# One fused attention and gated MLP kernel: block-diagonal M and z, statistics' loads in buffers of their own, first blocks' loads issued first

## The chip, the cores and the metric

The kernel runs on one core of one Trainium2 chip. The metric is device time in microseconds; lower is better. The version before was run three times: 676.85, 678.36 and 680.79 us, median 678.36 us. All inputs are float32 or float64 in HBM; the weights of the MLP are float64.

## The reference

Attention of 4 batches, 8 heads, 576 rows, 64 columns per head, mixed with a linear-attention memory, and then a gated MLP over 2304 rows of 512:

```python
scores = where(causal, -1e9, q @ k.T / sqrt(64))
a = exp(scores - max);  a /= a.sum(-1) + 1e-09
local = a @ v
q_p = where(q > 0, q, exp(q) - 1) + 1
mem_out = (q_p @ M_prev) / ((q_p @ z_prev) + 1e-06)
x = sigmoid(beta) * mem_out + (1 - sigmoid(beta)) * local
# rows of x are 8 heads x 64
xn = x / sqrt(mean(x * x) + 1e-06) * rms_g
g = xn @ w_gate
out = (silu(g) * (xn @ w_val)) @ w_out
```

## The kernel before

The 2304 rows are 18 blocks of 128. Blocks 0 and 1 are the first 128 rows of batch 0 and of batch 1; they need no earlier keys and are computed wholly in float32 (`n < NA`). All other blocks use float16 pairs (a high and a low half), whose scales come from statistics over k and v of a whole batch. Blocks go in pairs (chunks) through the MLP: `m_proj` multiplies a chunk's transposed, normalised rows `xT` with 12 column groups F of the weights; `m_act` makes the gated product; `m_down` multiplies with w_out. Chunk 0 is done in float32, with weights that were only just turned from float64 to float32.

The order on each engine is that of a scheduler at build time, which takes the calls in program order and with priorities (`tc.high_priority`). An engine runs its own list strictly in that order; so does SP, the queue that issues nearly all DMAs. Each DMA takes the next of eight semaphores, and waits for the DMA that had that semaphore before it.

What happens in the head of the program, with the names used below:

- `HORD` is a string that orders the first loads: q0 and k0 (`kv`, k and v) of block 0, M0 and M1 (the memory of batch 0 and 1, each loaded twice, into both halves of the partitions), w0 and w1 (the first weight pieces). `HP` is a priority for them; 0 is none.
- Weights: gate and val come in 24 pieces of 128 x 512 float64 (512 KB). `load_w` puts piece p in slot p mod 5 of a ring in the `wo` tile, and `paced` lets it start only once the conversion of piece p - 3 has begun. `f64_to_f32` converts a piece: one operation on ACT (L777), then two on DVE (L778, L779). A slot is free for piece p + 5 after the second one on DVE. w_out follows in 12 pieces of the same kind.
- `prep_qk32` transposes k and q of a block on PE (L351, `tp`), `phi_calc` makes phi(q), `prep_phi32` transposes it.
- `u_scores` multiplies q and k (L411, `sc`), `u_exp` takes the exponentials on ACT with their sums in `den`, `u_lo` transposes the result (L351 again, from `S`), `pv32` multiplies it with v (L582, `both<-kv`).
- `mem32` makes for each of 8 heads a product of 64 partitions with z (L558, `zn`, one column) and one with M (L570, `both<-wo`, 64 columns). `evac32` scales both by the two denominators and adds them; `x_norm` and `x_float` (L691, `xtp`) normalise and transpose the row block for the MLP.
- `all_stats(b)` for batches 0 and 1: `stat_blk` feeds each block's k and v to `gram` (L147, `csum<-kv`, `csum<-pre`), four products of 128 x 128 each, whose maximum DVE reads (L241). The blocks (b, 2) and (b, 3) are loaded for this alone by `load_pre`, into the tile `pre`; there is one buffer for it (`tag="res", bufs=1`). So each of these four loads (two DMAs each) waits until the products of the one before it are done.
- `gv_scales` uses the same `gram` on converted weights (`csum<-wgv`).

Of the kernel before, what the change touches and what calls it, by code (L numbers as in the profile page):

```python
# [9 lines left out]
F32 = mybir.dt.float32  # L10
F16 = mybir.dt.float16
# [5 lines left out]
ALU = mybir.AluOpType  # L17
# [4 lines left out]
LNP = 15.0 * math.log(2.0)  # L22
XSCALE = 2.0 ** 11
NEG = -1.0e38
HP = 0
HORD = "q0 k0 M0 w0 w1 q1 k1 M1"
LAG = 3
LAG0 = 8
NA = 2
HEAD0 = 1.0  # L30
ADD32 = "p"
# [27 lines left out]
def attn_memory_moe_kernel(  # L59
# [12 lines left out]
    nc = tc.nc  # L72
    B, D, H = M_prev.shape[:3]
# [158 lines left out]
    def stat_blk(b, i):  # L232
        if b < 2:
            r = slice(0, P) if i < NI else slice(b * TR, b * TR + TR)
            src = pre.pop((b, i)) if (b, i) in pre else stage[blk_of[(b, i)] if i < NI else NI * 2]
            for j in range(2):
                if i == 0:
                    csum["kv", b, j] = ps.tile([P, 512], F32, tag="out", name=f"csum{j}")
                gram(csum["kv", b, j], src[r, j], i == 0, i == NI)
                if i == NI:  # L240
                    nc.vector.tensor_reduce(  # L241
                        stt[b][:, j, 0:1], csum.pop(("kv", b, j))[:, :P], axis=AX.X, op=ALU.max
                    )
            return
        if i < NI:
            for j in range(2):
                square_acc(stage[blk_of[(b, i)]][:, j], stt[b][:, j, i : i + 1])
# [145 lines left out]
    def group(n):  # L393
        return max(1, 4 // (blocks[n][1] + 1)) if blocks[n][1] < 2 else 1
# [71 lines left out]
    def u_exp(n, h0):  # L466
        s, w, nm = Ssb[(n, h0)]
        G = group(n)
        if n < NA:
            if h0 % 4 == 0:  # L470
                den[n, h0 // 4] = tiny.tile([P, 2, 4], F32, tag="qsc", name="den", bufs=5)
            for g in range(G):
                v_ = s[:, g * w : (g + 1) * w]
                nc.scalar.activation(
                    v_, v_, AF.Exp, bias=nm[:, g : g + 1], scale=-1.0,
                    accum_out=den[n, h0 // 4][:, 1, (h0 + g) % 4 : (h0 + g) % 4 + 1],
                )
# [68 lines left out]

    t1s = {}

    def mem32(n, g4):

        b, i = blocks[n]
        if g4 == 0:
            z = ps.tile([P, 2, 4], F32, tag="sc", name="zn")
            for x in range(H):
                h, r = head32(x)
                if x % 4 == 0:
                    zt = z if x == 0 else ps.tile([P, 2, 4], F32, tag="sc", name="zn")
                nc.tensor.matmul(  # L558
                    zt[:, x // 4, x % 4 : x % 4 + 1], q32[n][r, 1, h // 2, :],
                    zz[r, b * H + h : b * H + h + 1], start=True, stop=True,  # L560
                )
                if x % 4 == 3:
                    nc.vector.scalar_tensor_tensor(
                        out=den[n, x // 4][:, 0], in0=zt[:, x // 4], scalar=1e-6,
                        in1=gsig[:, 0, four(n, x // 4)], op0=ALU.add, op1=ALU.mult,
                    )
        accs[n, g4] = ps.tile([P, 2, 4, D], F32, tag=f"a{g4}", name=f"both{n}_{g4}", bufs=1)
        for x in range(4 * g4, 4 * g4 + 4):
            h, r = head32(x)
            nc.tensor.matmul(  # L570
                accs[n, g4][:, 0, x % 4], q32[n][r, 1, h // 2, :], qst[("M", b)][r, h * D : h * D + D],
                start=True, stop=True,
            )
        if (n, g4) == (NA - 2 + b, 1):
            del held["M", b, 1]

    def pv32(n, h0, pt):
        b, i = blocks[n]
        for g in range(group(n)):
            x = h0 + g  # L580
            h = head32(x)[0]
            nc.tensor.matmul(  # L582
                accs[n, x // 4][:, 1, x % 4], pt[:, g, :], stage[blk_of[(b, 0)]][:, 1, h * D : h * D + D],
                start=True, stop=True,
            )

    def evac32(n, g4):
        f = den.pop((n, g4))
        nc.vector.scalar_tensor_tensor(
            out=f[:, 1], in0=f[:, 1], scalar=1e-9,  # L590
            in1=gsig[:, 1, four(n, g4)], op0=ALU.add, op1=ALU.mult,
        )
        nc.vector.reciprocal(f, f)
        if g4 == 0:
            t1s[n] = sb.tile([P, H, D], F32, tag="t1", name=f"t1_{n}")
        t2 = sb.tile([P, 2, 4, D], F32, tag="t2", name=f"t2_{n}", bufs=1)
        nc.vector.tensor_tensor(
            t2, accs.pop((n, g4)), f.unsqueeze(3).to_broadcast([P, 2, 4, D]), ALU.mult
        )
        (nc.vector if ADD32 == "d" else nc.gpsimd).tensor_tensor(  # L600
            t1s[n][:, four(n, g4), :], t2[:, 0], t2[:, 1], ALU.add
        )

    def mem_mm(n, g4):
        if n < NA:
            return mem32(n, g4)
        b, i = blocks[n]
        if g4 == 0:
            t1s[n] = sb.tile([P, H, D], F32, tag="t1", name=f"t1_{n}")
# [141 lines left out]

    def load_pre(b, i):

        pre[(b, i)] = sb.tile([P, 2, HD], F32, tag="res", name=f"pre{b}_{i}", bufs=1)
        for j in range(2):
            nc.sync.dma_start(out=pre[(b, i)][:, j], in_=qkv[blk_of[(b, i)], :, j, :])

    def load_wo(f):
        at = {0: 7, 1: 9, 2: 11, 3: 7, 4: 9, 5: 11, 7: 9, 9: 11}.get(f)
# [279 lines left out]
            load_w(*pcs[p])  # L1039
    load_kv(2), load_kv(3)  # L1040
    setup_consts()
    for n in range(2):
        prep_qk32(n)
        phi_calc(n)
        prep_phi32(n)
# [223 lines left out]
```

## Time and profile before

| what | value |
|---|---|
| median of 3 runs | 678.36 us (676.85 to 680.79) |
| span of the profiled execution | 677.3 us |
| PE busy | 623.5 us, 92% |
| DVE busy | 474.8 us, 70% |
| ACT busy | 384.1 us, 57% |
| POOL busy | 164.3 us, 24% |
| HBM read and written | 36.20 MB, 4.72 MB |

The profiled execution has no time of its own in the list of runs; its span is 1.1 us under the median of the runs, and this difference stands for what lies around a span. The page cuts the span in 40 slices of 16.9 us: PE's busy share is 5, 8, 9, 8, 9 tenths in the first five, and the granted TensorE clock is 9, 6, 5, 5, 8 tenths there; in the second half of the span both are at 9 nearly throughout.

### The profile page before, as it was taken

The page shows a single profiled execution, that of the slowest core. Times are in us where ns is not written, and L with a number is a line of the kernel's source. Part 1 is how long each engine was busy: PE and PEld are TensorE (multiplying, and loading weights), DVE is VectorE, ACT ScalarE, POOL GpSimd, SP SyncE. Part 2 cuts the span into 40 slices and gives each one's busy share as a digit, 9 for nine tenths or more (in the row PEclk, how much of TensorE's full clock was granted, in tenths as well). Part 3 has the DMA queues.
Part 4 walks back from the last instruction along what each step waited for, and adds up shares of the span by engine and source line. Part 5 has one row for each costly group of instructions (what it writes and reads, how often), then busy time and mean ns, then how long its engine had stood idle before and what let it go on. Part 6 is the DMA issues. An engine that isn't in the chain of part 4 may idle for free.

```text
span 677.3 us, 16070 instructions
## 1 busy us (share of the span) xinstructions
PE 623.5 (92%) x6152; PEld 489.4 (72%) x6152; DVE 474.8 (70%) x1448; ACT 384.1 (57%) x799; POOL 164.3 (24%) x239
## 2 busy tenths in 40 slices
PE   5898968899798969999899899989999999999997
PEld 4786857755686647778687777767787788887774
DVE  5556977897899776689668666877887676872221
ACT  3334655647778776665657656956557554542322
POOL 0001110131255324232143122522232221212111
PEclk9655988899999969999899999999999999999999
DMA  7745899933933777636466763285785454351001
GB/s 257 271 165 198 253 273 249 208 72 63 226 76 76 170 161 167 142 76 146 112 139 111 167 161 64 51 153 135 124 135 114 90 93 99 76 76 21 32 1 31
DMA packets 191660, 88.63 MB, mean 131 GB/s; under 512 B 174176, under 2 KB 174176, under 8 KB 191584
## 3 DMA queue, kind: packets, MB, share of 16 engines
q1 hardware_dynamic: 191136, 87.59, 56.2%
q8 instruction: 48, 0.79, 0.5%
q14 instruction: 28, 0.23, 0.1%
q10 hardware_dynamic: 448, 0.02, 0.0%
HBM read 36.20 MB, written 4.72 MB: 60 GB/s over the span
## 4 chain that ended last, share of the span: by engine, by line
PE 56%; DMA 19%; DVE 11%; ACT 7%; issue 4%; SPq 2%; POOL 1%; ACTq 0%; DVEq 0%; POOLq 0%
PE gv L858 26%; DMA PT<-P 6%; PE out L920 4%; PE out L921 4%; PE out L919 4%; DMA wo<-in_moe_w_out_dram 3%; DMA kv<-in_qkv_dram 3%; PE sc L418 3%; PE sc L445 2%; ACT junk L225 2%; DVE S L424 2%; DMA wo<-in_moe_w_gate_dram 2%; DMA qT<-row 2%; DVE P L500 1%; DMA wo<-in_moe_w_val_dram 1%
## 5 line engine op out<-in xcount | busy, mean ns | idle before, releaser
L858 PE MATMUL gv<-xT,wgv 128*128 128x256 f16 x2304 | 314.5, 274 | 1.3 <-DMA xT<-x 1.3
L858 PEld LDWEIGHTS <-wgv 128*128 128x128 f16 x2304 | 221.9, 98 | 38.4 <-DMA xT<-x 1.5
L890 POOL TENSOR_TENSOR h<-th,h 128x256 f16<-128x256 f32 x96 | 72.4, 754 | 263.1 <-ACT h L889 202.8
L482 ACT ACTIVATE S<-S,nm 128x256 f32<-128x256 f32 (+4 forms) x128 | 75.1, 608 | 47.9 <-DVE nm L432 34.6
L418 PE MATMUL sc<-kT,qT 128*128 128x128 f16 x608 | 84.1, 221 | 4.5 <-DMA qT<-qT 1.8
L500 DVE TENSOR_TENSOR P<-S,P 128x512 f16<-128x512 f32 (+2 forms) x84 | 64.6, 769 | 26.3 <-ACT P L487 25.7
L874 ACT ACTIVATE th<-gv,wt 128x256 f32<-128x256 f32 x96 | 44.8, 467 | 57.4 <-PE gv L858 53.4
L875 DVE SCALAR_TENSOR_TENSOR th<-th,gv 128x256 f32<-128x256 f32 x96 | 39.9, 415 | 52.7 <-ACT th L874 52.1
L424 DVE CUSTOM_DVE_ANT_0 S<-sc,mask,qsc 128x256 f32<-128x256 f32 (+3 forms) x112 | 62.2, 573 | 17.6 <-PE sc L418 14.1
L920 PE MATMUL out<-wo,h 128*128 128x512 f16 x192 | 73.2, 382 | 0.4 <-DVE wo L98 0.4
L921 PE MATMUL out<-wo,h 128*128 128x512 f16 x192 | 72.3, 381 | 0.0
L919 PE MATMUL out<-wo,h 128*128 128x512 f16 x192 | 72.1, 382 | 0.0
L487 ACT CAST P<-S 128x512 f16<-128x512 f32 (+2 forms) x100 | 59.6, 596 | 12.1 <-DMA PT<-P 10.8
L526 PE MATMUL loc<-v,PT 128*128 128x65 f16 x304 | 50.2, 195 | 14.3 <-DMA PT<-P 14.1
L889 ACT CAST h<-th 128x256 f16<-128x256 f32 x96 | 38.4, 400 | 43.9 <-DVE th L878 42.0
L418 PEld LDWEIGHTS <-qT 128*128 128x128 f16 x608 | 51.2, 98 | 10.6 <-issue 3.4
L851 PE MATMUL gv<-xT,wgv 128*128 128x256 f32 x192 | 47.8, 405 | 6.0 <-DVE h32e L878 6.0
L527 PE MATMUL loc<-v,PT 128*128 128x64 f16 x304 | 50.0, 195 | 0.0
L528 PE MATMUL loc<-v,PT 128*128 128x65 f16 x304 | 50.0, 195 | 0.0
L878 DVE SCALAR_TENSOR_TENSOR th<-th,wt,gv 128x256 f32<-128x256 f32 x96 | 45.8, 477 | 1.7
L660 POOL TENSOR_TENSOR t<-t,t 128x256 f32<-128x256 f32 x32 | 25.8, 806 | 86.0 <-DVE t L656 73.5
L851 PEld LDWEIGHTS gv<-xT,wgv 128*128 128x128 f32 x192 | 37.7, 202 | 12.3 <-DVE h32e L878 6.4
(216 smaller groups left out, 1141.5 us busy)
## 6 DMA issues: line engine op xcount, KB each, us to landing
kv<-in_qkv_dram SPq DMA_DIRECT2D x36, 256.0 KB, 3.6
wo<-in_moe_w_gate_dram SPq DMA_DIRECT2D x12, 512.0 KB, 5.5
wo<-in_moe_w_val_dram SPq DMA_DIRECT2D x12, 512.0 KB, 5.3
q<-in_qkv_dram SPq DMA_DIRECT2D x18, 256.0 KB, 3.0
wo<-in_moe_w_out_dram SPq DMA_DIRECT2D x8, 512.0 KB, 4.6
qT<-qT SPq DMA_DIRECT2D x32, 128.0 KB, 2.4
out_dram<-res SPq DMA_DIRECT2D x16, 256.0 KB, 2.3
pre<-in_qkv_dram SPq DMA_DIRECT2D x8, 256.0 KB, 3.0
```

Of the source, the lines that this page charges most:

```text
L418: nc.tensor.matmul(t[:, g * w + j * P : g * w + (j + 1) * P], qT[n][:, t2, h, :], kT[blk_of[(b, j)]][:, h, :], start=(t2 == 0), stop=(t2 = ...
L424: nc.vector.tensor_tensor_reduce(out=s[:, g * w : (g + 1) * w], in0=t[:, g * w : (g + 1) * w], in1=mask[:, m0 : m0 + w], scale=qsc[n][:, 5 ...
L482: nc.scalar.activation(v_, v_, AF.Exp, bias=nm[:, g : g + 1], scale=-1.0)
L487: nc.scalar.copy(p16[:, : G * w], s[:, : G * w])
L500: eng.tensor_tensor(p16[:, w : 2 * w], s[:, :w], p16[:, :w], ALU.subtract)
L526: nc.tensor.matmul(a, phi_, vhi, start=(j == 0), stop=False)
L851: nc.tensor.matmul(o, wgv[:, 1 + p, o0 : o0 + P], xT[0][:, cc, :], start=(cc == 0), stop=(cc == NC - 1))
L858: nc.tensor.matmul(o, lhs, xT[c][:, rhs, :], start=(cnt == 0), stop=(cnt == 3 * NC - 1))
L890: nc.gpsimd.tensor_tensor(h16[:, 1], th, h16[:, 0], ALU.subtract)
L919: nc.tensor.matmul(o, hh, whi, start=(f == 0), stop=False)
L920: nc.tensor.matmul(o, hh, wlo, start=False, stop=False)
L921: nc.tensor.matmul(o, hl, whi, start=False, stop=(f == NF - 1))
```

## The change

Four things are changed.

- **Loads.** `pre` gets a tile per load of k and of v, in the ten buffers of `v16`, which are empty at that time, so that none of its eight DMAs waits for a product. `HORD` now orders q0, k0, q1, k1, M0, M1, w0, w1, w2, with a high priority.
- **Statistics.** The `gram` products of batches 0 and 1 get a lower priority (-300).
- **Memory.** `pair_memory` clears on POOL a tile `Mpair` of 128 x 1024 floats and a `zpair` of 128 x 16, and `pair_M` copies M of two heads at a time onto the diagonal. `mem32` then needs 4 products with 128 partitions and 128 columns in place of 8, and 4 with z in place of 8, and does its scaling alone (`fm32`).
- **Accumulators.** Memory and local part of a float32 block lie in separate PSUM tiles, `evac32` scales only the local part, and adds it to `t1`.

```diff
-HP = 0
-HORD = "q0 k0 M0 w0 w1 q1 k1 M1"
+HP = 3000
+HORD = "q0 k0 q1 k1 M0 M1 w0 w1 w2"
...
-                gram(csum["kv", b, j], src[r, j], i == 0, i == NI)
+                with tc.high_priority(-300):
+                    gram(csum["kv", b, j], src[j][r], i == 0, i == NI)
...
+    def pair_memory():
+        mb = sb.tile([P, 2, NC, 2, D], F32, tag="xT", name="Mpair")
+        zb = sb.tile([P, 2, NC, 2], F32, tag="h16", name="zpair", bufs=4)
+        nc.gpsimd.memset(mb, 0.0)
+        nc.gpsimd.memset(zb, 0.0)
...
+    def pair_M(b):
+        m4 = qst["M", b].rearrange("p (c t e) -> p c t e", c=NC, t=2)
+        for t, r in ((0, slice(0, D)), (1, slice(D, 2 * D))):
+            nc.gpsimd.tensor_copy(pairs["M"][r, b, :, t, :], m4[r, :, t, :])
...
+        for c in range(NC):
             nc.tensor.matmul(
-                accs[n, g4][:, 0, x % 4], q32[n][r, 1, h // 2, :], qst[("M", b)][r, h * D : h * D + D],
-                start=True, stop=True,
+                acc[:, 2 * c : 2 * c + 2, :], q32[n][:, 1, c, :], pairs["M"][:, b, c], start=True, stop=True
             )
+        for c in range(NC):
+            nc.tensor.matmul(
+                z[:, 2 * c : 2 * c + 2], q32[n][:, 1, c, :], pairs["z"][:, b, c], start=True, stop=True
+            )
...
-        pre[(b, i)] = sb.tile([P, 2, HD], F32, tag="res", name=f"pre{b}_{i}", bufs=1)
+        pre[(b, i)] = []
         for j in range(2):
-            nc.sync.dma_start(out=pre[(b, i)][:, j], in_=qkv[blk_of[(b, i)], :, j, :])
+            t = sb.tile([P, H, VW], F16, tag="v16", name=f"pre{b}_{i}_{j}", bufs=10)
+            t = t.bitcast(F32).rearrange("p a b -> p (a b)")[:, :HD]
+            nc.sync.dma_start(out=t, in_=qkv[blk_of[(b, i)], :, j, :])
```

SP's list before, from its start, loads alone. The tile `wo` holds M and the weight pieces; kv8 is the block of last rows, kv2 and kv3 are the second blocks of the two batches.

```order
L205 DMA kv8_497<-in_qkv_dram 128x512 x2
L756 DMA pre0_2_518<-in_qkv_dram 128x512 x2
L220 DMA q0_96<-in_qkv_dram 128x512
L205 DMA kv0_98<-in_qkv_dram 128x512 x2
L214 DMA wo_84<-in_M_prev_dram 64x512 x2
L747 DMA wo_84<-in_moe_w_gate_dram 128x512 x2
L220 DMA q1_105<-in_qkv_dram 128x512
L205 DMA kv1_107<-in_qkv_dram 128x512 x2
L214 DMA wo_84<-in_M_prev_dram 64x512 x2
L747 DMA wo_84<-in_moe_w_gate_dram 128x512
L205 DMA kv2_113<-in_qkv_dram 128x512 x2
L205 DMA kv3_116<-in_qkv_dram 128x512 x2
```

Behind these come q2, a gate piece and a val piece, q3, a val piece, and then a `pre` load between every one to three pieces until all four are issued. SP's list of the change, from its start (lines are numbered anew):

```order
L220 DMA q0_96<-in_qkv_dram 128x512
L205 DMA kv0_98<-in_qkv_dram 128x512 x2
L220 DMA q1_101<-in_qkv_dram 128x512
L205 DMA kv1_103<-in_qkv_dram 128x512 x2
L214 DMA wo_84<-in_M_prev_dram 64x512 x4
L762 DMA wo_84<-in_moe_w_gate_dram 128x512 x3
L205 DMA kv8_491<-in_qkv_dram 128x512 x2
L773 DMA pre0_2_0_512<-in_qkv_dram 128x512
```

Behind this row stand the other seven `pre` DMAs. The list of the change from the last of them on:

```order
L773 DMA pre1_3_1_645<-in_qkv_dram 128x512
L205 DMA kv2_113<-in_qkv_dram 128x512 x2
L205 DMA kv3_116<-in_qkv_dram 128x512 x2
L220 DMA q2_198<-in_qkv_dram 128x512
L220 DMA q3_764<-in_qkv_dram 128x512
L762 DMA wo_84<-in_moe_w_gate_dram 128x512
L762 DMA wo_84<-in_moe_w_val_dram 128x512 x4
```

All eight `pre` DMAs now stand ahead of piece 3 (the fourth), and none between pieces; pieces 3 to 23 follow q3 without anything between them. Behind the last piece the list goes on as before: the transpose of kT0, kv4, and the w_out pieces.

DVE's list before, at the maxima of the first batch's sums (L241) and the conversions around them:

```order
L778 TENSOR_SCALAR wo_84<-wo_84 128x512
L589 SCALAR_TENSOR_TENSOR den_311<-den_311,gsig_85 128x4
L241 TENSOR_REDUCE stt0_495<-csum0_500 128x1
L355 COPY PT32_356<-tp_357 128x512
L779 SCALAR_TENSOR_TENSOR wgv_83<-wgv_83,wo_84 128x512
L241 TENSOR_REDUCE stt0_495<-csum1_505 128x1
L778 TENSOR_SCALAR wo_84<-wo_84 128x512
```

DVE's list of the change, from the same place on, through the maxima of both batches (L244 is the line of the maximum, L796 and L797 those of the conversion):

```order
L244 TENSOR_REDUCE stt0_489<-csum0_494 128x1
L589 RECIPROCAL fm32_351<-fm32_351 128x8
L796 TENSOR_SCALAR wo_84<-wo_84 128x512
L615 TENSOR_TENSOR t2_1_370<-loc1_363,den_314 128x256
L244 TENSOR_REDUCE stt0_489<-csum1_499 128x1
L591 TENSOR_TENSOR t1_1_354<-mem1_342,fm32_351 128x512
L797 SCALAR_TENSOR_TENSOR wgv_83<-wgv_83,wo_84 128x512
L796 TENSOR_SCALAR wo_84<-wo_84 128x512
L244 TENSOR_REDUCE stt1_611<-csum0_613 128x1
L796 TENSOR_SCALAR wo_84<-wo_84 128x512
L244 TENSOR_REDUCE stt1_611<-csum1_618 128x1
L797 SCALAR_TENSOR_TENSOR wgv_83<-wgv_83,wo_84 128x512 x2
```

The first L797 of this piece is piece 6, the last row pieces 7 and 8. Maxima of both batches stand here close together; those of the second batch moved forward, from the two sides of the end of piece 11's conversion to ahead of the end of piece 7's.

## Rows read from the trace of the kernel before

**Rows 1.** Stretches: length; PE, PEld, DVE, ACT, POOL busy; granted clock, DMA share, GB/s.
```profile
340.00:677.00 337.00, 327.89 (x3522) 257.13 (x3519) 216.87 (x637) 179.27 (x380) 84.10 (x125) 1.00 0.47 93
...
204.00:340.00 136.00, 121.48 (x1403) 94.54 (x1402) 105.08 (x317) 93.32 (x186) 42.93 (x55) 0.95 0.60 131
...
61.00:86.00 25.00, 23.52 (x151) 19.36 (x152) 22.70 (x72) 16.63 (x32) 3.82 (x7) 0.90 0.82 256
...
20.00:61.00 41.00, 38.86 (x196) 33.20 (x196) 20.42 (x61) 10.27 (x30) 3.78 (x6) 0.52 0.56 196
...
4.00:24.00 20.00, 13.04 (x87) 10.85 (x88) 13.04 (x53) 7.43 (x26) 0.25 (x1) 0.94 1.00 341
```

**Rows 2.** The chain that ended last, 78 to 150 us: start, duration, what.
```profile
88.97 4.50 DMA wo<-in_moe_w_out_dram
```

**Rows 3.** Line L777, first operation of a weight piece's conversion, from 60 us.
```profile
L777 ACT ACTIVATE wgv<-wo x13: 653/688/704, 61.4 to 83.3; 128x512 f32<-128x512 f32 x13
```

**Rows 4.** SP's instructions in order of time: start us, us, line, what.
```profile
0.79 0.90 SPq L205 DMA_DIRECT2D kv<-in_qkv_dram  x2
...
4.77 0.33 SPq L220 DMA_DIRECT2D q<-in_qkv_dram  x1
...
20.75 0.33 SPq L747 DMA_DIRECT2D wo<-in_moe_w_val_dram  x1
28.83 0.80 SPq L756 DMA_DIRECT2D pre<-in_qkv_dram  x2
...
44.17 0.81 SPq L756 DMA_DIRECT2D pre<-in_qkv_dram  x2
...
55.55 0.80 SPq L756 DMA_DIRECT2D pre<-in_qkv_dram  x2
```

**Rows 5.** What SP waited for, to 150 us: sum, times, longest.
```profile
SPq L756 <- PE csum L147: 13.9, 2, 7.9
SPq L756 <- PE tp L351: 7.7, 1, 7.7
```

**Rows 6.** DMA issues: times, size, median us from issue to landing.
```profile
kv<-in_qkv_dram SPq DMA_DIRECT2D x36, 256.0 KB, 3.6
wo<-in_moe_w_gate_dram SPq DMA_DIRECT2D x12, 512.0 KB, 5.5
```

**Rows 7.** PE in order of time: start us, us (with the drain), line, tiles, count.
```profile
7.92 0.58 PE L134 MATMUL allp<-ident,zq 128*1 128x128 f32 x2 [7.92 <-ACT junk L225]
...
13.34 1.89 PE L411 MATMUL sc<-k,q 64*128 64x128 f32 x16
...
17.16 0.63 PE L351 MATMUL tp<-ident,kv 128*128 128x128 f32 x4 [0.58 <-DMA kv<-in_qkv_dram]
...
20.68 0.40 PE L147 MATMUL csum<-kv 128*128 128x128 bf16 x4 [2.46 <-DMA kv<-in_qkv_dram]
...
33.12 2.05 PE L411 MATMUL sc<-k,q 64*128 64x128 f32 x8
...
59.88 0.61 PE L147 MATMUL csum<-kv 64*128 64x128 bf16 x4
...
64.97 2.29 PE L147 MATMUL csum<-wgv 128*128 128x128 bf16 x28
...
67.50 0.70 PE L851 MATMUL gv<-xT,wgv 128*128 128x256 f32 x2
```

**Rows 8.** PE's groups from 20 to 61 us, shapes apart: busy us, mean ns.
```profile
L558 PE MATMUL zn<-zz,q 64*128 64x1 f32 x32 | 7.9, 344 | 0.0
...
L570 PE MATMUL both<-wo,q 64*128 64x64 f32 x16 | 3.9, 425 | 0.0
L691 PE MATMUL xtp<-diag,t 128*128 128x128 f32 x8 | 3.1, 494 | 0.0
```

**Rows 9.** POOL's groups to 140 us, shapes apart: busy us, mean ns.
```profile
L600 POOL TENSOR_TENSOR t<-t 128x256 f32<-128x256 f32 x4 | 3.0, 754 | 42.8 <-DVE t L597 23.4 <-DVE den L589 19.4
...
L293 POOL COPY M<-zhl 128x16 f16<-128x16 f16 x2 | 0.6, 276 | 10.6 <-DVE cb L275 10.6
```

More of the change, by code (lines that the diff above doesn't have):

```diff
@@ L234, in stat_blk @@
             r = slice(0, P) if i < NI else slice(b * TR, b * TR + TR)
-            src = pre.pop((b, i)) if (b, i) in pre else stage[blk_of[(b, i)] if i < NI else NI * 2]
+            src = pre.pop((b, i)) if (b, i) in pre else [
+                stage[blk_of[(b, i)] if i < NI else NI * 2][:, j] for j in range(2)
+            ]
             for j in range(2):
@@ L470, in u_exp @@
             if h0 % 4 == 0:
-                den[n, h0 // 4] = tiny.tile([P, 2, 4], F32, tag="qsc", name="den", bufs=5)
+                den[n, h0 // 4] = tiny.tile([P, 4], F32, tag="qsc", name="den", bufs=5)
             for g in range(G):
@@ L475, in u_exp @@
                     v_, v_, AF.Exp, bias=nm[:, g : g + 1], scale=-1.0,
-                    accum_out=den[n, h0 // 4][:, 1, (h0 + g) % 4 : (h0 + g) % 4 + 1],
+                    accum_out=den[n, h0 // 4][:, (h0 + g) % 4 : (h0 + g) % 4 + 1],
                 )
@@ L547, in attn_memory_moe_kernel @@
     t1s = {}
-    def mem32(n, g4):
-        b, i = blocks[n]
[L552 to L569, printed above, removed]
+    pairs = {}
@@ new lines, in pair_memory @@
+    def pair_memory():
[4 more added lines that the diff above has]
+        for t, r in ((0, slice(0, D)), (1, slice(D, 2 * D))):
+            z4 = zz[r].rearrange("p (b c t) -> p b c t", b=B, t=2)
+            nc.gpsimd.tensor_copy(zb[r, :, :, t], z4[:, :2, :, t])
+        pairs["M"], pairs["z"] = mb, zb
+    def pair_M(b):
+        m4 = qst["M", b].rearrange("p (c t e) -> p c t e", c=NC, t=2)
+        for t, r in ((0, slice(0, D)), (1, slice(D, 2 * D))):
+            nc.gpsimd.tensor_copy(pairs["M"][r, b, :, t, :], m4[r, :, t, :])
+        del held["M", b, 1]
@@ L570, in mem32 @@
+    def mem32(n):
+        b, i = blocks[n]
+        z = ps.tile([P, H], F32, tag="sc", name="zn")
+        acc = ps.tile([P, H, D], F32, tag="a0", name=f"mem{n}", bufs=1)
+        for c in range(NC):
             nc.tensor.matmul(
-                accs[n, g4][:, 0, x % 4], q32[n][r, 1, h // 2, :], qst[("M", b)][r, h * D : h * D + D],
-                start=True, stop=True,
-            )
-        if (n, g4) == (NA - 2 + b, 1):
-            del held["M", b, 1]
+                acc[:, 2 * c : 2 * c + 2, :], q32[n][:, 1, c, :], pairs["M"][:, b, c], start=True, stop=True
+            )
+        for c in range(NC):
+            nc.tensor.matmul(
+                z[:, 2 * c : 2 * c + 2], q32[n][:, 1, c, :], pairs["z"][:, b, c], start=True, stop=True
+            )
+        f = tiny.tile([P, H], F32, tag="qsc", name="fm32", bufs=5)
+        nc.vector.scalar_tensor_tensor(
+            out=f, in0=z, scalar=1e-6, in1=gsig[:, 0], op0=ALU.add, op1=ALU.mult
+        )
+        nc.vector.reciprocal(f, f)
+        t1s[n] = sb.tile([P, H, D], F32, tag="t1", name=f"t1_{n}")
+        nc.vector.tensor_tensor(t1s[n], acc, f.unsqueeze(2).to_broadcast([P, H, D]), ALU.mult)
@@ L577, in pv32 @@
     def pv32(n, h0, pt):
         b, i = blocks[n]
+        if h0 == 0:
+            accs[n] = ps.tile([P, 2, 4, D], F32, tag="a1", name=f"loc{n}", bufs=1)
         for g in range(group(n)):
@@ L582, in pv32 @@
             nc.tensor.matmul(
-                accs[n, x // 4][:, 1, x % 4], pt[:, g, :], stage[blk_of[(b, 0)]][:, 1, h * D : h * D + D],
+                accs[n][:, x // 4, x % 4], pt[:, g, :], stage[blk_of[(b, 0)]][:, 1, h * D : h * D + D],
                 start=True, stop=True,
@@ L589, in evac32 @@
         nc.vector.scalar_tensor_tensor(
-            out=f[:, 1], in0=f[:, 1], scalar=1e-9,
-            in1=gsig[:, 1, four(n, g4)], op0=ALU.add, op1=ALU.mult,
+            out=f, in0=f, scalar=1e-9, in1=gsig[:, 1, four(n, g4)], op0=ALU.add, op1=ALU.mult,
         )
@@ L594, in evac32 @@
         if g4 == 0:
[L595 to L602, printed above, removed]
+            t1s["t2"] = sb.tile([P, 2, 4, D], F32, tag="t2", name=f"t2_{n}", bufs=1)
+        t2 = t1s["t2"][:, g4]
+        acc = accs[n] if g4 == 0 else accs.pop(n)
+        nc.vector.tensor_tensor(t2, acc[:, g4], f.unsqueeze(2).to_broadcast([P, 4, D]), ALU.mult)
+        part = t1s[n][:, four(n, g4), :]
+        (nc.vector if ADD32 == "d" else nc.gpsimd).tensor_tensor(part, part, t2, ALU.add)
     def mem_mm(n, g4):
         if n < NA:
-            return mem32(n, g4)
+            return mem32(n) if g4 == 0 else None
         b, i = blocks[n]
@@ L752, in load_pre @@
     def load_pre(b, i):
-        pre[(b, i)] = sb.tile([P, 2, HD], F32, tag="res", name=f"pre{b}_{i}", bufs=1)
+        pre[(b, i)] = []
         for j in range(2):
-            nc.sync.dma_start(out=pre[(b, i)][:, j], in_=qkv[blk_of[(b, i)], :, j, :])
+            t = sb.tile([P, H, VW], F16, tag="v16", name=f"pre{b}_{i}_{j}", bufs=10)
+            t = t.bitcast(F32).rearrange("p a b -> p (a b)")[:, :HD]
+            nc.sync.dma_start(out=t, in_=qkv[blk_of[(b, i)], :, j, :])
+            pre[(b, i)].append(t)
     def load_wo(f):
@@ L1041, in attn_memory_moe_kernel @@
     setup_consts()
+    pair_memory()
+    for b in range(2):
+        pair_M(b)
     for n in range(2):
```

## The prediction

> **What bounds the kernel now.** I read the stretches first. In the second half PE is busy 327.9 of 337 us at full clock, and from 204 to 340 us 121.5 of 136: there nothing but less PE work or an earlier start can help. From 20 to 61 us PE is also busy, 38.9 of 41 us, but at a clock of 0.52, while DVE is half idle, ACT more, and the DMA share is 0.56 [rows 1]. So the head is where time lies, and the question is what ends it.
>
> What ends it is the stream of weight pieces. From 61.4 to 83.3 us 13 conversions begin, one in (83.3 - 61.4) / 12 = 1.83 us [rows 3]; right behind the last one the chain that ends last runs through the w_out pieces, which come through the same ring [rows 2]. Ahead of 61 us the pieces were held: SP issues a piece at 20.75 and then stands at the `pre` loads until 28.83, later again until 44.17 and until 55.55 [rows 4], because `pre` has one buffer and its products were still to do [rows 5]; the two sums, 13.9 + 7.7, make 21.6 us of SP standing. The products themselves waited in PE's list among small float32 products at half clock.
>
> **The weight stream after the change.** SP's new list has ahead of piece 3, counted in units of 256 KB: 6 for q0, k0, v0, q1, k1, v1, 2 for M, 6 for three pieces, 2 for kv8, 8 for `pre`, 4 for kv2 and kv3, 2 for q2 and q3, together 30 or 7.86 MB. From 4 to 24 us, with DMAs queued behind each other, the trace moved 341 GB/s [rows 1]. At that rate 7.86 MB take 23 us; with 3 us ahead of it (SP's first DMA goes out at 0.79 [rows 4], and a load takes 3.6 us to land [rows 6]) they are in at 26 us. Piece 3 (0.52 MB, 1.5 us) is in at 27.5. Twenty more at 1.83 us: the last conversion begins at 27.5 + 36.5 = 64.0, **19.3 us** earlier than 83.3. Bounds: at 341 GB/s all along a piece takes 1.54 us and the last begins at 58.3 (25.0 us earlier); at the 256 GB/s of the stretch from 61 to 86 us [rows 1] it takes 2.05 us, and the last begins at 68.5 (14.8 earlier). I take 1.83, since it is measured on this very stream, its pacing and its conversions together.
>
> **What may hold the stream.** The conversion ends on DVE, which keeps its order. In the new order the end of piece 7's conversion stands behind the maxima of both batches, so behind all 80 statistic products on PE; piece 12 needs the slot of piece 7. Undisturbed, piece 12 is issued when the conversion of piece 9 begins, at 27.5 + 6 x 1.83 = 38.5. If PE ends the statistics later than 38, every microsecond more is lost.
>
> When does PE end them? Before the change the work from the first waiting statistic product at 20.68 to the last at 60.48 (59.88 and its 0.6) took 39.8 us [rows 7], nearly all of it busy. Up to 20.68 PE had worked from 7.92 with gaps of 0.58 and 2.46 us [rows 7], so 9.7 us, and q0 had gone out only at 4.77, behind kv8 and `pre` [rows 4]. Now q0 and k0 go out first and land by some 5 to 6 us, q1 and kv1 right behind: 6 + 9.7, I let PE reach this point at 16. The block-diagonal tiles save in the stretch half of the products with z (7.9 us busy together, so 3.9) and put 4 products with M of 128 columns (at the price of `xtp`, four products in 3.1) in place of 8 of 64 columns (3.9): 4.7 us off [rows 8], 35.1 left. At half clock the statistics end at 16 + 35 = **51**. At full clock the same kind of product is 2.2 times as fast (`sc` took 1.89 us for 16 records at 13.34, and 2.05 for 8 at 33.12), and 28 products of the statistics' size took 2.29 us, 0.08 each [rows 7]: then the work fits into some 17 us, and data set its end: the second batch's sums need the accumulators whose maxima stand behind the conversion of piece 6, at 33.0, and 40 products at 0.08 follow: **36**. No row says which, so I take the middle, 43.5. With 0.3 us for the maximum on DVE that costs 43.8 - 38.5 = **5.3 us** (0 at one end, 12.8 at the other).
>
> Row and rule differ here. The rows show PE busy for 41 us at 0.52, the level of 1.2 GHz [rows 1]. The Trainium skill ("TensorE: Matmul & The Clock Gate", section on the HAM clock gate) says that the throttled level is the idle one and that sustained activity releases it; by that rule a head with fewer and larger products would run at 2.4 GHz, and the sum would have no loss of 5.3 us. The rows say that being busy by the profile is not enough; so I do not take the rule whole.
>
> **Smaller parts.** The saved products count only through the 43.5 above: if nothing waited for PE in the head, they would be covered by the weight stream and worth nothing; with PE the bound there they are the 4.7 us already in it. POOL's four copies of M and the clearing of `Mpair` are not in the trace. A copy of 64 x 256 lies between the 0.28 us of the small copy and the 0.75 of a 128 x 256 addition [rows 9]; two of them come after M0 has landed, so 0.6 to 1.5 us. Clearing 1024 columns costs at most four such additions, 3 us, and runs while the first loads fly. PE reaches the product with M at about 13 us, M0 is the seventh and eighth load and in by some 11.5: I take no wait; the upper end, 1.5 us, is within the spread of the 43.5. The eight semaphores make k1 wait for the small first load of ACT's queue, as q0 had to wait until 4.77 [rows 4]: this is in the 16. The split accumulators leave DVE the same columns, one scaling of 512 and two of 256 for two of 512, on an engine that is half idle there: nothing.
>
> **Behind the weights.** SP's list behind piece 23 is as before, and each step there waits for the ring or for a step before it [rows 2], so it moves as a whole. PE is not in its way: its projections began at 67.5 [rows 7] and begin now around 49, before piece 23 is in. So the shift is carried to 204 us and by PE to the end.
>
> **Sum.** 19.3 - 5.3 = 14.0 us off the span: 677.3 - 14.0 = 663.3. The median of the runs is 1.1 over the span: **664 us**. A measurement of this kernel can tell some 0.5%, 3.4 us, from no change: faster means under 675.0, slower over 681.8.
>
> **Rivals.**
> - *Clock released early* (the rule above): statistics end at 36, the stream is not held, gain 19.3: **659**. For it: PE was at the faster pace at 13.34, after dense products [rows 7], and the new list has longer dense runs of statistics. Against: 41 us at 0.52 in a list much like it.
> - *Half clock all through*: statistics end at 51, loss 12.8, gain 6.5: **672**. For it the same 41 us; against, the waits that led to it (2.46 us for kv2 [rows 7]) are smaller.
> - *Slower: DVE's order starves the ring.* Statistics of both batches need kv2 and kv3, which now land behind all `pre` loads, after 26 to 28 units, at about 23 us. If PE's list in effect stands until then and needs the old 39.8 us from there, they end at 62.8; piece 12 is issued at 63.1, is there 5.5 us later [rows 6], and 11 more at 1.83 make the last conversion begin at 88.7, 5.4 us later than now: **684**. It decides from 57.4 us on, where the last conversion is back at 83.3. Against it: blocks 0 and 1 do not need these loads, and stand ahead.
> - *Nothing left of it.* The scheduler also moves work behind 100 us: transposes, products with M and POOL's subtractions change places. PE's idle time from 204 to 340 is 136 - 121.5 = 14.5 us [rows 1]; were it doubled, the gain would be gone: **678**. Nothing in the changed lists looks like a longer chain.
>
> **How the numbers follow.** My forecast 0.46, clock released early 0.26, half clock 0.14, nothing left 0.09, starved ring 0.05. The first three are faster: 0.86; same 0.09; slower 0.05. The range takes in the first three with the bounds of a piece's time (the 1.54 us end would take 5.7 us more off 659): 653 to 675, leaving out the last two.
>
> **What would show it.** The last gate or val conversion should begin near 69 us (64 if the stream is free, 77 if PE stays at half clock); SP should have no wait at a `pre` load; the last statistic product should end near 43, and the projections begin before 50. The clock between 15 and 45 us decides between the first three. The chain of the w_out pieces should look as before, some 14 us earlier. I am wrong if the last conversion is early and the end is not, or if SP waits for DVE at pieces 8 to 12 for long.

## The result, and the profile after

The changed kernel takes **660.24 us** (median of four runs, 656.52 to 661.33) against 678.36 us for the kernel before on the same chip: a ratio of 0.9717, with a 95% interval of 0.9675 to 0.9759, so 18 us faster. 664 was forecast, with a range of 653 to 675. The profiled execution took 659.51 us, and its span is 657.7 us. Each ratio, here and below, is to runs of the kernel before on the same chip and leaves out executions more than 1.5% above the fastest of their kernel, while medians are of all executions.

The stretches of the changed kernel, columns as in [rows 1]:

```profile
4.00:24.00 20.00, 17.27 (x110) 14.43 (x110) 15.78 (x78) 9.85 (x40) 2.88 (x9) 0.93 0.96 343
20.00:61.00 41.00, 38.71 (x265) 32.52 (x266) 34.72 (x112) 21.84 (x49) 6.74 (x14) 0.83 0.87 302
61.00:86.00 25.00, 15.85 (x95) 13.26 (x93) 20.02 (x53) 14.83 (x28) 5.35 (x4) 0.86 0.96 242
204.00:340.00 136.00, 122.94 (x1489) 97.47 (x1488) 103.88 (x313) 89.46 (x181) 41.35 (x59) 0.96 0.72 139
340.00:657.00 317.00, 311.67 (x3297) 244.01 (x3294) 206.64 (x604) 169.91 (x358) 77.05 (x110) 1.00 0.47 93
```

From 20 to 61 us PE is busy as long as before (38.71 of 41 us), but at a clock of 0.83 where it was 0.52; DVE does 34.72 us of work there in place of 20.42, and the DMA rate is 302 GB/s in place of 196. Behind 204 us nothing of note has changed. So the gain lies in the head, as forecast. The pages give the busy time of the whole span, before and after:

```profile
PE 623.5 (92%) x6152; PEld 489.4 (72%) x6152; DVE 474.8 (70%) x1448; ACT 384.1 (57%) x799; POOL 164.3 (24%) x239
PE 608.9 (93%) x6120; PEld 476.6 (72%) x6120; DVE 476.7 (72%) x1450; ACT 382.8 (58%) x799; POOL 167.5 (25%) x247
```

Of the 19.6 us by which the span is shorter, PE's busy time makes 14.6, and its idle time (677.3 - 623.5 = 53.8 and 657.7 - 608.9 = 48.8) makes 5.0.

The conversions of the 24 gate and val pieces, as in [rows 3] but from the first on (first and last begin at 13.6 and 65.8 us):

```profile
L795 ACT ACTIVATE wgv<-wo x24: 657/674/698, 13.6 to 65.8; 128x512 f32<-128x512 f32 x24
```

The last one begins 17.5 us earlier than before. The chain that ended last runs behind it through a w_out piece, as in [rows 2], 18.9 us earlier:

```profile
70.08 3.61 DMA wo<-in_moe_w_out_dram
```

SP in order of time, which answers to [rows 4]:

```profile
0.79 0.40 SPq L220 DMA_DIRECT2D q<-in_qkv_dram  x1
...
11.50 7.33 SPq L773 DMA_DIRECT2D pre<-in_qkv_dram  x8
...
32.21 7.20 SPq L762 DMA_DIRECT2D wo<-in_moe_w_gate_dram  x4
42.96 4.67 SPq L762 DMA_DIRECT2D wo<-in_moe_w_val_dram  x4
```

All eight `pre` loads go out in one run, and no PE product holds them. There is still one hold of the stream, between 39.4 and 42.96 us. What SP waited for, to 150 us (as [rows 5]), then the same from 39.3 to 43 us alone, and DVE and ACT in order of time at the hold:

```profile
SPq L762 <- ACT wgv L795: 21.5, 15, 4.6
SPq L762 <- DVE wgv L797: 7.4, 5, 2.3
```

```profile
SPq L762 <- DVE wgv L797: 2.2, 1, 2.2
SPq L762 <- ACT wgv L795: 1.4, 1, 1.4
```

```profile
40.68 0.28 DVE L244 TENSOR_REDUCE stt<-csum 128x1 f32<-128x128 f32 x1
40.88 1.28 DVE L797 SCALAR_TENSOR_TENSOR wgv<-wgv,wo 128x512 int32<-128x512 int32 x2
```

```profile
36.92 0.66 ACT L795 ACTIVATE wgv<-wo 128x512 f32<-128x512 f32 x1 [0.59 <-DMA wo<-in_moe_w_gate_dram]
40.51 0.63 ACT L225 ACTIVATE junk<-t 128x512 bf16<-128x512 f32 x1 [2.92 <-POOL t L617]
...
42.27 1.23 ACT L795 ACTIVATE wgv<-wo 128x512 f32<-128x512 f32 x2
```

SP stood 2.2 us until DVE had ended piece 7's conversion, behind the last maximum at 40.68, as forecast, and then 1.4 us for ACT: the normalisation of block 1 stands ahead of piece 9's conversion there and waits for POOL, and the pace rule (a piece starts once the conversion three before it has begun) holds piece 12.

PE at the places of [rows 7]: the last statistic products, and the first projection.

```profile
39.80 0.40 PE L147 MATMUL csum<-kv 64*128 64x128 bf16 x4
...
46.73 3.72 PE L869 MATMUL gv<-xT,wgv 128*128 128x256 f32 x16
```

They ended at 60.5 and began at 67.5 before.

### The profile page after: what moved, and what is told of

The parts are those of the page before. It is cut to its first block, busy times and chain, and to the rows that moved or that the text cites. A ratio compares the mean times of both kernels' runs of the same rounds, so it can differ in the third digit from the quotient of the medians.

```text
span 657.7 us, 16005 instructions
## 1 busy us (share of the span) xinstructions
PE 608.9 (93%) x6120; PEld 476.6 (72%) x6120; DVE 476.7 (72%) x1450; ACT 382.8 (58%) x799; POOL 167.5 (25%) x247
## 4 chain that ended last, share of the span: by engine, by line
PE 51%; DVE 15%; DMA 15%; ACT 9%; issue 5%; SPq 3%; POOL 0%; ACTq 0%; DVEq 0%; POOLq 0%
PE gv L876 25%; PE out L937 4%; PE out L938 4%; PE out L939 4%; DMA PT<-P 3%; DMA kv<-in_qkv_dram 3%; DVE S L427 2%; PE sc L421 2%; ACT junk L225 2%; DVE P L503 2%; DMA rawo<-in_moe_w_out_dram 2%; PE sc L448 2%; DMA wo<-in_moe_w_out_dram 1%; PE out L929 1%; DMA wo<-in_moe_w_val_dram 1%
## 5 line engine op out<-in xcount | busy, mean ns | idle before, releaser
L503 DVE TENSOR_TENSOR P<-S,P 128x512 f16<-128x512 f32 (+2 forms) x84 | 62.5, 745 | 25.1 <-ACT P L490 24.5
L869 PE MATMUL gv<-xT,wgv 128*128 128x256 f32 x192 | 50.3, 421 | 4.6 <-DVE h32e L896 4.6
L869 PEld LDWEIGHTS gv<-xT,wgv 128*128 128x128 f32 x192 | 39.8, 213 | 11.7 <-DVE h32e L896 4.7
```

Source lines behind the costliest of these rows:

```text
L503: eng.tensor_tensor(p16[:, w : 2 * w], s[:, :w], p16[:, :w], ALU.subtract)
L869: nc.tensor.matmul(o, wgv[:, 1 + p, o0 : o0 + P], xT[0][:, cc, :], start=(cc == 0), stop=(cc == NC - 1))
```

## The experiments

All runs in one table. The clock is the granted clock of the stretch from 4 to 68 us. Then follow, in us of the profiled execution: the end of the last statistic product, the begin of the first projection, of the last gate or val conversion, and of the first float16 projection, and the span.

| kernel | median | ratio to before (95%) | clock | statistics | projections | last conversion | first float16 | span |
|---|---|---|---|---|---|---|---|---|
| before | 678.4 | 1 | 0.65 | 60.5 | 67.5 | 83.3 | 165.4 | 677.3 |
| changed | 660.2 | 0.972 (0.968 to 0.976) | 0.89 | 40.2 | 46.7 | 65.8 | 148.3 | 657.7 |
| undo_buffers | 658.9 | 0.970 (0.965 to 0.974) | 0.92 | 51.2 | 42.2 | 71.0 | 150.9 | 658.7 |
| undo_order | 668.0 | 0.983 (0.977 to 0.989) | 0.79 | 42.1 | 60.8 | 71.6 | 155.8 | 665.8 |
| undo_priority | 661.4 | 0.974 (0.970 to 0.979) | 0.96 | 36.7 | 44.1 | 64.5 | 146.9 | 659.5 |
| undo_memory | 676.4 | 0.998 (0.995 to 1.000) | 0.76 | 51.3 | 56.2 | 67.3 | 166.0 | 672.4 |
| undo_mem_prio | 662.5 | 0.979 (0.973 to 0.985) | 0.81 | 46.2 | 55.7 | 67.0 | 149.8 | 658.6 |
| split_products | 663.3 | 0.978 (0.972 to 0.984) | 0.87 | 44.5 | 55.2 | 67.2 | 152.4 | 663.2 |
| pace4 | 662.0 | 0.976 (0.970 to 0.982) | 0.97 | 37.6 | 43.9 | 61.4 | 157.6 | 666.6 |
| only_buffers | 690.0 | 1.020 (1.014 to 1.027) | 0.72 | 49.3 | 72.8 | 83.3 | 175.2 | 686.4 |
| only_order | 680.2 | 0.997 (0.993 to 1.001) | 0.63 | 63.0 | 63.5 | 84.3 | 166.5 | 680.6 |
| only_memory | 664.1 | 0.979 (0.971 to 0.987) | 0.84 | 44.1 | 52.7 | 67.6 | 155.1 | 664.5 |
| order_memory | 660.4 | 0.972 (0.965 to 0.979) | 0.95 | 50.2 | 41.1 | 70.0 | 147.3 | 657.7 |
| warm_mem | 665.9 | 0.983 (0.976 to 0.990) | 0.84 | 45.9 | 52.8 | 67.0 | 148.9 | 662.5 |

The profiled execution of pace4 is the longest of its four (668.55 us of 659.55 to 668.55), that of only_order a long one (682.28 of 671.99 to 684.74); their medians are the better measure.

**One part undone at a time.** The theory that I began with (T) is that of the prediction: SP's waits at the statistics' loads set the weight stream, and its end sets the time. Against it stood R: what PE has to do in the head.

The buffers undone (undo_buffers):

```diff
...
+        t = sb.tile([P, 2, HD], F32, tag="res", name=f"pre{b}_{i}", bufs=1)
...
-            t = sb.tile([P, H, VW], F16, tag="v16", name=f"pre{b}_{i}_{j}", bufs=10)
...
```

> The changed kernel, with the four second-and-third-block loads of the statistics again in one buffer for all. Theory T (the end of the weight stream sets the time; SP standing at these loads sets the stream): SP waits again at them for statistic products, together over 10 us, the last gate or val conversion begins between 75 and 84 us (changed kernel 65.8), and the time grows by as much: 669 to 678 us. Theory R (the gain comes from less and earlier work of PE in the head): the waits at these loads are short, because the products come earlier, the last conversion begins before 70 us and the time stays under 664 us.

What SP waited for in this kernel, to 150 us:

```profile
SPq L772 <- PE csum L147: 8.7, 2, 5.5
```

The waits are back, though 8.7 us and not over 10, the last conversion is 5.2 us later, and the time is the same as with the change. T expected 669 or more and is refuted: with the rest of the change in place, the buffers are not what the gain hangs on.

The load order undone (undo_order):

```diff
-HP = 3000
-HORD = "q0 k0 q1 k1 M0 M1 w0 w1 w2"
+HP = 0
+HORD = "q0 k0 M0 w0 w1 q1 k1 M1"
```

> The changed kernel, with the old order of the first loads: the statistics' loads (10 of 256 KB, 2.6 MB, 7.7 us at 341 GB/s) go out ahead of q0. Theory T: the same bytes stand ahead of piece 3, so it lands at about the same time, but everything that PE does with block 0 and 1 starts some 5 to 7 us later, the normalisation of block 1 on ACT (which stands ahead of piece 9's conversion) with it; the last conversion begins between 67 and 73 us, and the time is 661 to 667 us. Theory R (PE's work in the head sets the time): the whole of the 5 to 7 us is seen, 665 to 668 us, with the projections of chunk 0 begun after 52 us (changed kernel 46.7) and PE without a long wait behind them.

The projections begin 14.0 us later, the last conversion 5.8 us (as T has it), and 7.7 us of time come back: within R's figures, and 1 us over T's. By the page PE is busy 606.2 us of the 665.8, so the loss is idle time of PE (59.6 us in place of 48.8), not a slower PE.

The priority undone (undo_priority): `gram` without `tc.high_priority(-300)`.

> The changed kernel, with the statistics' products at their old priority. Theory T: PE's list hardly changes, the last conversion begins within 1.5 us of 65.8 and the time is within 2 us of the changed kernel, 658 to 662 us. Theory R: statistic products that wait for late loads stand again ahead of small products of block 0 and 1; PE idles over 3 us more in the first 45 us, and the time is 664 us or more.

1.2 us, inside the spread: nothing, as T has it.

The memory part undone (undo_memory), 16 products of 64 partitions a block and the shared accumulators:

```diff
...
-                acc[:, 2 * c : 2 * c + 2, :], q32[n][:, 1, c, :], pairs["M"][:, b, c], start=True, stop=True
+                accs[n, g4][:, 0, x % 4], q32[n][r, 1, h // 2, :], qst[("M", b)][r, h * D : h * D + D],
...
```

> The changed kernel, with the old memory products (16 of 64 partitions a block, no block-diagonal tiles) and the old shared accumulators. Theory T: PE has some 4 to 5 us more work in the head, so the normalisation of block 1 and piece 9's conversion come up to 4.7 us later, the stream makes part of it up again: last conversion between 66 and 70 us, time 660 to 664 us. Theory R: PE's saved work is the gain; all of the 4.7 us, doubled at half clock, comes back: 668 us or more.

Nearly all of the gain is gone, although the last conversion is only 1.5 us later than with the change. T gives 660 to 664 and fails by 12 us; R's "or more" holds, but 4.7 us of work do not make 16. Two readings of this kernel show where they are. First PE's clock, over 30 us (columns as in [rows 1]):

```profile
20.00:50.00 30.00, 29.63 (x155) 26.68 (x156) 19.90 (x56) 11.16 (x30) 3.97 (x8) 0.50 0.79 280
```

With the change the half clock ended at 35 us:

```profile
22.00:34.00 12.00, 11.98 (x66) 10.66 (x65) 7.69 (x29) 4.37 (x13) 2.37 (x6) 0.50 0.92 330
34.00:36.00 2.00, 2.00 (x16) 1.72 (x15) 1.03 (x3) 1.01 (x2) 0.00 (x0) 0.83 0.99 348
36.00:52.00 16.00, 13.73 (x124) 10.94 (x123) 15.77 (x45) 10.24 (x22) 3.62 (x7) 1.00 0.80 267
```

Then PE around 150 us in the kernel with the memory part undone, in order of time:

```profile
151.17 2.74 PE L917 MATMUL out<-wo,h32v 128*128 128x512 f32 x6
153.75 0.19 PE L529 MATMUL loc<-v,PT 128*128 128x65 f16 x1
...
154.47 2.82 PE L917 MATMUL out<-wo,h32v 128*128 128x512 f32 x6
165.96 2.29 PE L864 MATMUL gv<-xT,wgv 128*128 128x256 f16 x10 [8.67 <-DMA xT<-x]
```

Its list has 24 attention products (`loc`) of block 3 behind most of the second block's `out` products; so the block's transpose is late, and PE waits 8.67 us for it. From the first `out` product (132.3 us) to the first float16 projection pass 33.6 us, with the change 21.5.

**Clock or work.** Next I asked whether the clock, the work itself, or the accumulators cost this. Theory B: the clock in the head sets when the statistics end, and the time follows.

undo_mem_prio is undo_memory without the lower priority of the statistics:

> The changed kernel with the old memory products and accumulators, and with the statistics' products at their old priority as well. In the kernel with the old memory products alone PE's clock stood at 0.50 from 20 to 50 us, the statistics ended at 51.3 and the first transpose of k began at 72.3 (changed kernel 0.50 from 22 to 34, 40.2 and 61.5), while the last weight conversion came only 1.5 us later; the time was 676.4. In the kernel with the old priority alone the clock was back at 1.00 by 30. Theory B (the time follows the chain from the statistics over the scales and k's transposes to the attention of blocks 2 and 3, and the clock in the head sets when that starts): with the statistics' dense products earlier in PE's list the clock is back before 40, the first transpose of k begins before 66 and the time is 666 us or less. Theory E (what counts is the extra work of the old memory products and the shared accumulators themselves, whatever the clock): the first transpose still begins after 70 and the time stays at 672 us or more.

The time is B's, the milestone is not: the clock was back at 30 us but fell again at 40 (0.81 over the head), the first transpose of k came at 72.3 as without this step, and yet the time is 14 us less. So the work of the old products is not what costs (E is refuted), and the transpose of k is not what the time follows. The first `out` product comes at 127.6 in place of 132.3, and the 24 products stand ahead of the second block's `out` products here, so most of the 14 us is that place in the list.

Read against the kernel before, this run says more: it differs from it by the buffers and the load order alone, and takes 662.5 us. Neither of these two gains anything by itself (only_buffers and only_order below), and together they give 16 us without the block-diagonal tiles. Its products are those of the kernel before, and PE is busy 10.0 us less with them (623.5 before):

```profile
PE 613.5 (93%) x6152; PEld 480.1 (73%) x6152; DVE 471.6 (72%) x1448; ACT 383.2 (58%) x799; POOL 162.5 (25%) x239
```

split_products keeps the tiles and accumulators of the change, but makes 8 products and 8, not 4 and 4:

```diff
...
-                acc[:, 2 * c : 2 * c + 2, :], q32[n][:, 1, c, :], pairs["M"][:, b, c], start=True, stop=True
+                acc[:, h], q32[n][:, 1, h // 2, :], pairs["M"][:, b, h // 2, h % 2], start=True, stop=True
...
```

> The changed kernel, with 8 products of 64 columns and 8 of one column for the memory of a block, out of the same block-diagonal tiles, instead of 4 and 4; accumulators and everything on DVE and POOL as in the changed kernel. Theory B: 16 more small products among the first two blocks hold the clock at 0.50 longer, until 40 us or later, the statistics end after 45 and the first transpose of k begins after 66; the time is 666 us or more. Theory F (the loss of the kernel with the old memory products came from the shared accumulators and the longer scaling, not from PE): 16 products of 0.2 to 0.4 us cost at most 6 us on PE, half of it covered; the first transpose begins before 65 and the time is under 664 us.

Between the two: 663.3 us, statistics at 44.5, first transpose of k at 69.3. The clock did not stay low from 20 on: it was at 1.00 until 32, and at 0.50 from 34 to 42. This run does not separate B from F; it shows that 16 products more a block, with the tiles and accumulators of the change, cost some 3 us and not 16. PE has as many products as before, and is busy as long as with the change:

```profile
PE 609.0 (92%) x6152; PEld 478.7 (72%) x6152; DVE 474.9 (72%) x1450; ACT 383.7 (58%) x799; POOL 167.3 (25%) x247
```

So the number of products is not what makes PE's busy time shorter.

pace4 (`PACE = 4`) lets the weights run one piece further ahead:

> The changed kernel, with the weight pieces allowed one more piece ahead (a piece may start when the conversion four before it has begun, not three). Theory T (the weight stream's end sets the time): the stream had 21.5 us of SP waiting for conversions, the last conversion begins 3 to 8 us earlier than 65.8, and the time falls by as much, to 652 to 657 us. Theory B: the stream's end moves, but the chain of the statistics does not start earlier (first transpose of k within 2 us of 61.5); the time stays within 3 us of the changed kernel, 657 to 663 us.

The last conversion begins 4.4 us earlier, and no time is gained. With undo_buffers, where it begins 5.2 us later and no time is lost, this says that between 61 and 71 us the stream's end does not set the time.

**Each part alone, on the kernel before.** only_buffers has nothing but the buffers:

> The kernel before, with nothing changed but the buffers of the statistics' loads: each in one of its own. Theory T: SP no longer stands 21.6 us at these loads, the last conversion begins between 66 and 73 us instead of 83.3, and the time falls by as much, to 661 to 668 us. Theory B: PE's order and its half clock are as before, so the statistics still end after 50 and the first transpose of k begins after 72 us (before 81.0); the time falls by less than 9 us and is 670 us or more, however early the last conversion is.

11 us *slower* than before: against T, and within B's "670 us or more", though B had no such loss in view. PE is busy 622.9 us of the 686.4, as long as before; its idle time is 9.7 us more. The 21.6 us of SP at `pre` [rows 5] are gone, and others have come in their place:

```profile
SPq L749 <- DVE wgv L784: 19.7, 9, 8.8
SPq L749 <- ACT wgv L782: 19.1, 9, 7.3
...
SPq L749 <- DVE den L595: 7.4, 1, 7.4
```

PE at 0.50 from 36 to 56 us is what DVE waits for:

```profile
51.78 3.60 PE L147 MATMUL csum<-wgv 128*128 128x128 bf16 x32
```

Behind these 32 products stand those with z of block 1, and behind the `den` that they feed stands a conversion in DVE's list. The last conversion begins at 83.3, as before.

only_order and only_memory have the load order alone and the block-diagonal part alone, order_memory both (the change without its buffers and without the priority). Theory O: the gain needs the load order.

> The kernel before, with nothing changed but the order of the first loads (that of the changed kernel, with its priority); one buffer for the statistics' loads as before. Theory O (the order of the loads is what the gain needs: blocks 0 and 1 and the gate pieces start early, the rest follows): the work of block 1 ends before 52 us (before 60.2), the projections begin before 60, the last conversion before 74, and the time is 660 to 667 us. Theory T as predicted (SP's waits at the statistics' loads are the cost): SP still stands over 12 us at these loads, the last conversion begins after 76 and the time is 671 us or more.

> The kernel before, with nothing changed but the block-diagonal tiles and the separate accumulators. Theory O: the old load order keeps the work of block 1 and the statistics late (projections begin after 62 us), and the time is 671 us or more. Theory E (less work of PE in the head is worth its time, at half clock twice): the 4.7 us and their effect on the clock bring the statistics forward by 6 us or more, the projections begin before 60 and the time is 668 us or less.

> The changed kernel without its buffers for the statistics' loads and without their lower priority: load order and block-diagonal tiles alone. Theory O: within 3 us of the changed kernel, 657 to 663 us, with SP standing up to 15 us at the statistics' loads but no piece late by more than 6 us. Theory T as predicted: the last conversion begins after 74 us and the time is 668 us or more.

O is refuted by the first two. For only_order T's figures came true (680.2 us, last conversion at 84.3, 18.9 us at the `pre` loads); for only_memory E's did (664.1 us, projections at 52.7), and for order_memory O's did and T's did not. The order alone gives nothing that can be measured; in its profiled execution PE was at half clock throughout the head, and SP stood 18.9 us at the `pre` loads:

```profile
20.00:62.00 42.00, 36.59 (x186) 31.94 (x185) 22.13 (x66) 13.32 (x41) 5.59 (x10) 0.50 0.58 196
```

```profile
SPq L756 <- PE csum L147: 18.9, 3, 10.9
```

The block-diagonal part alone, tiles and accumulators together, takes 13 to 15 us off, with the buffer, the order and the waits at `pre` (2.9 us are left of them) as they were. With both, the time is that of the whole change.

**The clock by itself.** The last run adds work, and nothing else, to undo_memory:

```diff
+                for _ in range(WARM * (b == 0 and i == 1)):
+                    gram(csum["kv", b, j], src[j][r], False, False)
```

> The kernel with the old memory products and accumulators (676.4 us, clock at 0.50 from 20 to 50 us), with 32 products more: the statistics' products of the first batch's second block are made five times over, without the lower priority, so that 20 of them stand close together from about 28 us on (the statistic counts that block five times; nothing else is changed). They are 3.4 us of work at half clock (8 such products took 0.86 us there). Theory C (the half clock of the head is what the old memory products cost; it follows what PE runs, not how much): the clock rises to 1.00 within 4 us of these products, the half clock in the head is less than 22 us in place of 30.7, the statistics end before 48 us in place of 51.3 although there are more of them, and the time falls to 668 us or less. Theory W (PE's work in the head is what costs): 32 products more make it 2 to 4 us slower, 677 us or more, and the clock stays at 0.50 until 50.

PE at these products, and the stretches around them:

```profile
29.09 1.94 PE L148 MATMUL csum<-kv 128*128 128x128 bf16 x20
```

```profile
26.00:30.00 4.00, 4.00 (x27) 4.00 (x27) 2.19 (x8) 1.29 (x8) 0.72 (x1) 0.50 1.04 412
30.00:32.00 2.00, 2.00 (x28) 1.83 (x26) 0.79 (x2) 1.06 (x3) 0.92 (x2) 0.89 0.30 121
32.00:36.00 4.00, 4.00 (x43) 3.68 (x41) 3.55 (x7) 1.46 (x3) 0.57 (x1) 1.00 0.68 217
```

The clock goes from 0.50 to 1.00 at these products. With 32 products more, the statistics end 5.4 us earlier, the projections begin 3.4 us earlier, the first `out` product 4.9 us (127.4), and the time is 10.5 us less: C holds, W fails. Not all of the 10.5 us is the clock's: the 24 `loc` products stand ahead of the second block's `out` products in this kernel's list, so the 12 us at 154 to 166 are gone too, and 7 us came back behind (from the first float16 projection to the end of the span it takes 513.6 us, in undo_memory 506.4). By the pages PE is busy 614.1 us of 662.5, with 32 products more, and 618.4 of 672.4 in undo_memory: of the 9.9 us of span, 4.3 are busy time, and 5.6 idle time of PE. What the faster clock gave here is nearer to the 4.9 us of the first `out` product than to the 10.5.

## Why the prediction was right, and where it was not

**The sum.** 664 against 660.2: the sign came true and the time lies in the range, though nearer to the rival "clock released early" (659) than to the likeliest case. That the sum came out is in part luck. 14.0 us off the span were forecast and 19.6 came: the forecast took off 5.3 for a hold that cost nothing on top, and had nothing for 2.5 us behind the shift.

**The pieces' stream** (19.3 us) measured 17.5. Its step was right almost to the digit: piece 3's conversion began at 28.9 (27.5 forecast), and 20 steps to 65.8 make 1.84 us each (1.83).

**The hold** (5.3 us) is the term that was mis-sized. It was there: 5.35 us between piece 8's conversion at 36.92 and piece 9's at 42.27, on DVE behind piece 7 for 2.2 us of SP's time, as forecast, and then on ACT for 1.4, at the normalisation of block 1, which the sum did not have. But it cost the end nothing beyond the 1.84, since the pieces behind it came every 1.68 us ((65.79 - 42.27) / 14). The 1.83 had been measured on a stretch with the same ring and pace and with gaps of its own, so a hold was counted twice. The last statistic product ended at 40.2, against 43.5.

**What the stream's delay came from** is the step that failed: that the pieces stood "because `pre` has one buffer and its products were still to do", so that the gain is the time of these waits. The waits were real, but they were waits for PE at half clock, and the span got shorter by PE's busy time (14.6 us) more than by its idle time (5.0). Taken away alone they come back on ACT and DVE (only_buffers, 690); kept, they shrink to 6 to 9 us and cost nothing once PE is fast (undo_buffers 658.9, order_memory 660.4).

**The smaller parts** failed with it: the saved products were to count only through the statistics' end, for 4.7 us at most. The memory part alone gives 13 to 15 us (only_memory), and not by its fewer products, since PE's busy time is the same with the old number (split_products). What moved was the clock, from 0.65 to 0.84 over the head, and with it the last conversion, from 83.3 to 67.6. The *rival "clock released early"* was nearest by its number (659) and in kind, but the clock came late: the half clock ended at 35 us, and the statistics at 40 where it had 36. The Trainium skill ("TensorE: Matmul & The Clock Gate", section on the HAM clock gate) has the low level as that of an idle engine, which sustained activity releases. These runs agree with half of it: 20 products close together raised it, but 29.63 us busy of 30 by the profile did not, as in the kernel before [rows 1]. That fewer and larger products bring it about was the prediction's own step beyond the rule, and no run shows it by itself.

**The shift behind the weights** was to be carried whole: the first float16 projection came 17.1 us earlier, and the end of the span 19.6. The 2.5 us more lie in the lists behind, where kernels differ anyhow: from the first float16 projection to the end the 14 kernels took 506 to 514 us.

**The other rivals.** "DVE's order starves the ring" (684) did not happen in the change. In only_buffers DVE's order did hold the ring, at 690, though not for the rival's reason, late kv2 and kv3: the statistics ended at 49.3 there, where it had 62.8. "Nothing left of it", through lists moved behind 100 us, is what undo_memory shows for 12 us.

How the whole change's gain divides among its parts is not settled, since they do not add up: the load order alone gives nothing, the buffers alone lose 11 us, and both together win 16. By kind it is 14.6 us of PE's busy time and 5.0 of its idle time. The busy time follows the clock: in the three kernels with a head clock of 0.72 or less PE is busy 623 to 626 us, in undo_memory (0.76) 618, in the other ten (0.79 or more) 602 to 614, with 6120 to 6184 product records in all of them. The idle time does not: it is 45 to 60 us in all but only_buffers (64), and it is what undo_order loses. One rival is left. The three kernels with the slowest head are also the three whose last conversion begins at 83 to 84 us, while the others begin it between 61 and 72. No run has a fast head and a late stream, so whether a late stream alone would hold the end is open. That the clock moves the time was shown by adding work (warm_mem), together with a change of the list. What raised it in each kernel was not isolated: the memory part did, the buffers with the load order did, and so did 32 more products. What holds the first float16 projection at 147 us when the clock is up and the stream early (pace4, undo_priority) was not tried.

## What to carry to other kernels

When a queue stands at a load, ask how fast the engine runs whose products free the buffer before buying more buffers: here the buffers alone cost 11 us, the memory part alone won 13 to 15, and buffers and load order without it won 16. Divide a gain into busy and idle time of the engine that is nearly always busy, before giving it to a wait that is gone. Read the granted clock stretch by stretch, and compare busy time only between stretches at the same clock. A pace that was measured on a stretch already contains that stretch's holds; do not add them again. And where a scheduler sets the lists, test a part alone and undone, since one group of products moved behind another cost 12 us far from the edit.

## What the runs showed of the hardware

PE stayed at 0.50, the 1.2 GHz level, for 30 us while it was busy 29.63 of them (undo_memory, 20 to 50 us): with float32 products of 1 to 128 columns and transposes, and for 8.8 us with 59 statistic products in bf16, 13 of them in one run of 1.59 us at 42.54. It rose to 1.00 at 20 statistic products in 1.94 us (warm_mem); adding 32 products took 4.3 us off PE's busy time there. In only_order the level fell to 0.50 between 14 and 16 us, with PE busy throughout these 2 us and the 4 before them. Clearing `Mpair` took 0.95 us by the profile, less than the 3 allowed for it, and three of the copies of M took 1.44 us; POOL in order of time, in the changed kernel:

```profile
0.87 0.95 POOL L558 MEMSET Mpair<- 128x1024 f32 x1
...
9.43 1.44 POOL L569 COPY Mpair<-wo 64x256 f32<-64x256 f32 x3 [1.90 <-DMA wo<-in_M_prev_dram]
```
